# A searched start order, a shorter Newton step and casts on VectorE in a fused attention and MLP kernel

**Chip, cores, metric.** One core of one Trainium2 chip. The metric is the device time of one execution in microseconds (us), as the median of several executions. Lower is better. TensorE is called PE, its weight loads PEld, VectorE DVE, ScalarE ACT, GpSimd POOL, SyncE SP. An `ACTq`, `SPq` or `POOLq` line is an engine's queue of instructions, where it issues DMAs.

## The reference, cut to what matters

```python
q, k, v: (8 batches, 12 heads, 448 rows, 64)    g_q, g_k: (64,)
q_n = q / sqrt(mean(q*q) + 1e-6) * g_q          # the same for k with g_k
attn = softmax(q_n @ k_n.T / 8)                 # per head, 448 x 448
x = (attn @ v) in token order                   # 3584 x 768
h = x @ w_in                                    # w_in 768 x 2048
out = (h * sigmoid(1.702 * h)) @ w_out          # w_out 2048 x 768, out 3584 x 768, fp32
```

The input is random. A pair is two heads of one batch; a batch has six pairs, and the MLP of a batch can start only when all six are done.

## The kernel before

Every piece of work is a task with an engine, an estimated duration, what it depends on, and a key. While the program is built, a list scheduler walks through modelled time. On each engine it emits the ready task with the smallest key. On the chip only the order per engine and the semaphores remain: a modelled start time does not hold anything back there (c1_order below issued its first `w_in` chunk at 1.82 us, where its table of start times has 12.24).

The tasks of a pair `i` are named by letters: `L` loads, `S` square on ACT, `R` reduction on DVE, `Q0` and `Q` the reciprocal root by Newton's method, `N` norm, `T` turn (transpose) on PE, `KQ` and `K` copies of the turned rows out of PSUM (the memory in which PE leaves its results), `C` scores, `E` exponentials on ACT, `V` cast of the values, `P` their product, `O` division, `B` and `X` the turn back and its copy. `F` is a group of the first MLP product, `Y` of the second, `WI` and `WO` chunks of the weights.

```python
def rsqrt(grp):                        # DVE for pair 0, POOL for the others
    eng = nc.vector if grp[0] == 0 else nc.gpsimd
    eng.tensor_tensor(out=yf.bitcast(I32), in0=magic[:SS, :m], in1=t.bitcast(I32), op=ALU.subtract)
    for _ in range(2):                 # 1 + 2 x 4 operations
        eng.tensor_tensor(out=t, in0=yf, in1=yf, op=ALU.mult)
        eng.tensor_tensor(out=t, in0=t, in1=x, op=ALU.mult)
        eng.tensor_scalar(out=t, in0=t, scalar1=-0.5, scalar2=1.5, op0=ALU.mult, op1=ALU.add)
        eng.tensor_tensor(out=yf, in0=yf, in1=t, op=ALU.mult)

def norm(i, gi):                       # always POOL
    nc.gpsimd.tensor_tensor(out=row_ring[i % N_QKN]..., in0=raw[i]..., in1=y..., op=ALU.mult)

def vcast(i):                          # always POOL
    nc.gpsimd.tensor_tensor(out=vx[:, :, :D], in0=vr, in1=ones..., op=ALU.mult)

# ... the gains are loaded from SP's queue, keys such as i - 4.5 are set by hand,
# ... three PSUM banks rotate for turns and MLP groups, w_out comes in four chunks of 512 rows
od.add(("S", i, j), "ACT", 950 / len(parts) + 100, lambda ..., i - 4.5, deps=[("L", i, w) ...])
od.add(("F", b, m), "PE", KI * 189, lambda b=b, m=m: first(b, m), key,
       deps=[("X", b * NP + p) for p in range(NP)] + [("WI", m // 4), last], ...)
```

## Time and profile before

| | before |
|---|---|
| device time, median of 3 (lowest to highest) | 456.48 us (455.66 to 456.92) |
| span of the profiled run, granted clock | 455.0 us, 0.968 |
| first exponential | 14.36 us |
| first group of the first MLP product (called T below) | 59.72 us |
| end of PE's last matmul | 449.68 us |

T is the number to read. From T on PE has nearly no idle time (1.0 us in all), and from T to PE's end it takes 389.96 us. So the start is where this kernel can be shortened. A score group in PE's timeline (`sc`, 4 matmuls) is a handy thermometer: in before it takes 0.59 us at full clock (at 50.42) and 0.99 at half clock (at 44.34). I call PE warm at full clock and cold at half clock.

### The profile page before, as it was taken

To read this page: it belongs to the slowest core of one execution; us is meant where nothing else is said; L and a number is where in the kernel's file an instruction comes from. 1 tells how busy PE (TensorE), PEld (TensorE's weight loads), DVE (VectorE), ACT (ScalarE), POOL (GpSimd) and SP (SyncE) were. 2 spreads that over 40 slices of the span, in tenths; PEclk is the share of its full clock that TensorE was granted. 3 is DMA by queue.
4 is the path that set the end of the run, shared out by engine and by line. 5 is a ranking of instruction groups with operands and counts; after the bars stand their busy time and mean duration, and the time that the engine had idled before them with its cause. 6 is when DMAs were issued, how large, how long until landed. Compare 5 with 4: busy or idle time off the path is not lost.

```text
span 455.0 us, 9525 instructions
## 1 busy us (share of the span) xinstructions
PE 423.0 (93%) x3728; PEld 244.4 (54%) x3728; DVE 211.9 (47%) x453; ACT 319.2 (70%) x463; POOL 193.2 (42%) x309
## 2 busy tenths in 40 slices
PE   0676799999999999999999999999999999999995
PEld 0343555566555655556556655555556555565563
DVE  5664678864663347624564326632551135404400
ACT  4665798887887878877887878976786667514411
POOL 3997797565436364445445534535443000000000
PEclk9965789999999999999999999999999999999999
DMA  8999999787555875566738576454213431021022
GB/s 199 235 245 246 254 262 245 151 183 197 139 117 133 192 184 155 124 148 152 190 94 195 146 184 164 121 139 130 55 39 80 99 84 22 12 79 36 0 71 70
DMA packets 95341, 63.35 MB, mean 139 GB/s; under 512 B 54336, under 2 KB 91712, under 8 KB 95296
## 3 DMA queue, kind: packets, MB, share of 16 engines
q1 hardware_dynamic: 89808, 56.22, 51.0%
q0 software_dynamic: 5248, 6.29, 7.8%
q8 instruction: 29, 0.48, 0.4%
q10 hardware_dynamic: 240, 0.23, 0.2%
q14 instruction: 16, 0.13, 0.1%
HBM read 45.61 MB, written 11.01 MB: 124 GB/s over the span
## 4 chain that ended last, share of the span: by engine, by line
PE 86%; DMA 8%; DVE 2%; ACT 2%; SPq 1%; issue 0%; ACTq 0%; DVEq 0%
PE op L505 32%; PE gp L482 32%; PE o L345 12%; PE sc L334 10%; DMA raw<-in_k_dram 5%; DMA raw<-in_q_dram 2%; DMA gq<-in_g_q_dram 1%; ACT att L338 1%; DVE obs L356 1%; DVE ssq L252 0%; SPq L241 0%; PE ot_ps L368 0%; PE t_ps L305 0%; DVE g L497 0%; DVE rcp L355 0%
## 5 line engine op out<-in xcount | busy, mean ns | idle before, releaser
L338 ACT ACTIVATE att<-sc 112x896 bf16<-112x896 f32 x192 | 167.3, 914 | 22.3 <-PE sc L334 21.1
L505 PE MATMUL op<-w_out_s,g 128*128 128x384 bf16 x896 | 162.8, 326 | 0.0
L482 PE MATMUL gp<-xt,w_in_s 128*128 128x448 bf16 x768 | 160.5, 353 | 0.2
L289 POOL TENSOR_TENSOR row<-raw,rs 112x512 bf16<-112x512 f32 x96 | 98.0, 1043 | 40.9 <-DMA qk<-row 38.4
L345 PEld LDWEIGHTS <-att 112*128 112x128 bf16 x1536 | 79.2, 101 | 55.3 <-issue 23.3
L497 DVE SCALAR_TENSOR_TENSOR g<-th,gp 128x448 bf16<-128x448 f32 x128 | 78.5, 618 | 60.6 <-ACT th L491 60.4
L505 PEld LDWEIGHTS <-g 128*128 128x128 bf16 x896 | 79.7, 97 | 48.4 <-issue 4.4
L345 PE MATMUL o<-vx,att 112*128 112x65 bf16 x1536 | 95.2, 200 | 5.4 <-DVE obs L356 2.9
L482 PEld LDWEIGHTS <-w_in_s 128*128 128x128 bf16 x768 | 68.9, 98 | 57.9 <-issue 4.2
L491 ACT ACTIVATE th<-gp 128x448 f32<-128x448 f32 x128 | 69.8, 546 | 37.8 <-PE gp L482 37.4
L296 POOL TENSOR_TENSOR vx<-vraw,ones 112x512 bf16<-112x512 f32 x48 | 50.0, 1042 | 100.5 <-PE o L345 87.4
L252 DVE TENSOR_REDUCE ssq<-sq 112x16 f32<-112x1024 f32 (+1 forms) x50 | 58.6, 1174 | 38.9 <-ACT sq L246 36.7
L355 DVE RECIPROCAL rcp<-o 112x4 f32<-112x4 f32 x96 | 17.4, 181 | 105.9 <-PE o L345 105.5
L334 PE MATMUL sc<-qk 64*112 64x448 bf16 x384 | 61.3, 394 | 5.7 <-ACT att L338 4.3
L246 ACT ACTIVATE sq<-raw 112x1024 f32<-112x1024 f32 (+1 forms) x50 | 51.0, 1023 | 19.2 <-DMA raw<-in_k_dram 17.0
L515 ACT ACTIVATE osb<-op 128x384 f32<-128x384 f32 x56 | 27.4, 490 | 50.5 <-PE op L505 46.9
L356 DVE TENSOR_TENSOR obs<-o,rcp 112x256 bf16<-112x256 f32 x96 | 40.8, 425 | 3.3
L334 PEld LDWEIGHTS <-qk 64*112 64x112 bf16 x384 | 18.9, 131 | 22.8 <-issue 17.2
L324 ACT ACTIVATE qk<-qk,gG 128x448 bf16<-128x448 bf16 x36 | 24.1, 668 | 0.0
L305 PE MATMUL t_ps<-ident,row 112*128 112x112 bf16 x96 | 9.7, 262 | 12.9 <-POOL row L289 12.9
L305 PEld LDWEIGHTS <-row 112*128 112x128 bf16 x96 | 7.2, 123 | 15.9 <-POOL row L289 14.5
L276 POOL TENSOR_TENSOR rs<-magic,seed 112x48 int32<-112x48 int32 (+1 forms) x16 | 4.5, 280 | 23.3 <-DVE seed L267 20.9
(31 smaller groups left out, 78.8 us busy)
## 6 DMA issues: line engine op xcount, KB each, us to landing
raw<-in_q_dram SPq DMA_DIRECT2D x48, 224.0 KB, 3.8
vraw<-in_v_dram SPq DMA_DIRECT2D x48, 224.0 KB, 3.7
raw<-in_k_dram SPq DMA_DIRECT2D x47, 224.0 KB, 4.0
w_in_s<-in_moe_w_in_dram POOLq DMA_DIRECT2D x4, 768.0 KB, 13.5
w_out_s<-in_moe_w_out_dram POOLq DMA_DIRECT2D x4, 768.0 KB, 11.6
out_dram<-osb SPq DMA_DIRECT2D x8, 336.0 KB, 3.0
out_dram<-osb SPq DMA_DIRECT2D x8, 288.0 KB, 2.7
out_dram<-osb SPq DMA_DIRECT2D x8, 240.0 KB, 2.8
```

Source lines behind the costliest of these rows:

```text
L246: nc.scalar.activation(out=sq_of[i][:SS, part], in_=raw[i][:SS, part], func=ACT.Square)
L252: nc.vector.reduce_sum(out=ssq_of[g0][:SS, i - g0, part], in_=sq_of[i][:SS, part], axis=AX.X)
L289: nc.gpsimd.tensor_tensor(out=row_ring[i % N_QKN][:SS, gi].rearrange("p n (h d) -> p h n d", h=2), in0=raw[i][:SS, gi], in1=y[:SS, a, gi]. ...
L296: nc.gpsimd.tensor_tensor(out=vx[:, :, :D], in0=vr, in1=ones[:SS, :].to_broadcast([SS, 2 * NS, D]), op=ALU.mult)
L334: nc.tensor.matmul(sc[:SS, hp, :S], lhsT=qk_ring[i % N_KZ][r, 1, kc, :], rhs=qk_ring[i % N_KZ][r, 0], start=True, stop=True)
L338: nc.scalar.activation(out=att_ring[i % N_ATT][:SS, kc, :, :S], in_=scs.pop((i, kc))[:SS, :, :S], func=ACT.Exp)
L345: nc.tensor.matmul(os_[i, hp][:, qs, :], lhsT=att_ring[i % N_ATT][:SS, kc, hp, qs * SS:qs * SS + WIN], rhs=vx_ring[i % N_V][:SS, hp, kc, : ...
L356: nc.vector.tensor_tensor(out=obs[i][:SS, :, hp, :], in0=o[:SS, :, :D], in1=rcp[:SS, :].to_broadcast([SS, NS, D]), op=ALU.mult)
L482: nc.tensor.matmul(ps[:, :], lhsT=w_in_s[:, ki, m * 128:(m + 1) * 128], rhs=xT[b][:, ki, :], start=(ki == 0), stop=(ki == KI - 1))
L491: nc.scalar.activation(out=th[:, :], in_=gps[b, m][:, :], func=ACT.Tanh, scale=0.851)
L497: nc.vector.scalar_tensor_tensor(out=g_of[b // 2][:, m, lo:lo + S], in0=ths.pop((b, m))[:, :], scalar=1.0, in1=gps.pop((b, m))[:, :], op0= ...
L505: nc.tensor.matmul(ops[bp, tm, hf][:, :], lhsT=g_of[bp][:, ko, tm * 128:(tm + 1) * 128], rhs=w_out_s[:, ko, hf * HALF:(hf + 1) * HALF], st ...
```

## The change

The intent is to bring T forward. It has five parts, and two smaller edits that stand in the last line of the diff:

- The order of the first pairs was searched offline. The keys of some 300 tasks and the start times of the loads stand as tables in the kernel, and the scheduler's model of the DMA was refined for that search.
- Newton's step is shorter (six DVE operations instead of nine for pair 0), and pair 0 is normed on DVE.
- The values of pairs 0 to 5 are cast on DVE.
- `w_out` is loaded by column halves, and the gains from ACT's queue.
- A hook for filler matmuls is added with its factor at zero. So neither kernel runs any filler.

```diff
+    def fill(idle):                    # called ahead of each PE task until the first MLP group
+        for _ in range(int(idle * FILL / 110)):
+            nc.tensor.matmul(banks[2][:, :256], lhsT=ident[:, :], rhs=zeros[:, :], start=True, stop=True)
+    FILL = 0.0
+        t.key = KEYS.get(name, key)    # KEYS and AT: two tables, about 80 lines, cut here
+        t.after, t.at, t.takes = tuple(deps), AT.get(name, at), takes
 ... seed: the halving and the sign are folded into two tensor_scalar, rsqrt:
         for _ in range(2):
-            eng.tensor_tensor(out=t, in0=yf, in1=yf, op=ALU.mult)
+            eng.tensor_tensor(out=t, in0=yg, in1=yg, op=ALU.mult)
             eng.tensor_tensor(out=t, in0=t, in1=x, op=ALU.mult)
-            eng.tensor_scalar(out=t, in0=t, scalar1=-0.5, scalar2=1.5, ...)
-            eng.tensor_tensor(out=yf, in0=yf, in1=t, op=ALU.mult)
+            if eng is nc.vector:
+                eng.scalar_tensor_tensor(out=yg, in0=t, scalar=1.5, in1=yg, op0=ALU.add, op1=ALU.mult)
+                continue
 ... norm
-        nc.gpsimd.tensor_tensor(
+        eng = nc.vector if i == 0 else nc.gpsimd
+        eng.tensor_tensor(
 ... vcast
+        if i < NP:
+            nc.vector.tensor_copy(out=vx[:, :, :D], in_=vr)
+            return
 ... load_g
-                nc.sync.dma_start(out=t[lo:lo + 64, :], ...)
+                nc.scalar.dma_start(out=t[lo:lo + 64, :], ...)
 ... load_out: hf, r = c // 2, c % 2
-            out=w_out_s[:, 4 * c:4 * c + 4, :],
+            out=w_out_s[:, 8 * r:8 * r + 8, hf * HALF:(hf + 1) * HALF],
 ... the turn is split into its two halves; two PSUM banks rotate before the first MLP group, three after
```

## The prediction

> **What bounds the kernel now.** I read the page's shares first, then its slices, then a table of stretches, then the timelines of the stretch that stood out.
>
> ```profile
> PE 423.0 (93%) x3728; PEld 244.4 (54%) x3728; DVE 211.9 (47%) x453; ACT 319.2 (70%) x463; POOL 193.2 (42%) x309
> ...
> PE   0676799999999999999999999999999999999995
> ...
> PEclk9965789999999999999999999999999999999999
> DMA  8999999787555875566738576454213431021022
> ```
>
> PE is full from the seventh slice on. The loss is in the first six slices (to 68 us) and in the last. The stretches, whose columns after the window are length, then PE, weight loads, DVE, ACT and POOL busy, granted clock, DMA share and GB/s:
>
> ```profile
> 30.00:40.00 10.00, 6.97 (x80) 5.49 (x78) 5.37 (x16) 2.04 (x3) 7.37 (x9) 0.50 1.18 245
> 40.00:50.00 10.00, 6.99 (x59) 4.05 (x58) 3.61 (x10) 7.34 (x10) 9.24 (x17) 0.50 1.16 256
> ...
> 100.00:150.00 50.00, 49.88 (x457) 28.50 (x456) 25.30 (x54) 40.61 (x61) 23.84 (x37) 1.00 0.61 146
> ```
>
> From 100 us PE is the bound and nothing else matters. From 30 to 50 us PE has few instructions, at half clock, and ACT is nearly idle. PE's timeline shows when the MLP starts:
>
> ```profile
> 59.37 0.56 PE L368 MATMUL ot_ps<-ident,obs 112*128 112x112 bf16 x4
> 59.72 1.73 PE L482 MATMUL gp<-xt,w_in_s 128*128 128x448 bf16 x6
> ```
>
> The first gp group needs the transposed outputs of all six pairs of batch 0; the sixth arrives at 59.4. From there MLP work fills every gap, and PE has under 2 us of idle time until it ends at 449.7. So the end is the start of the MLP plus fixed PE work plus a fixed 5.3 us tail. ACT's timeline says why the start is so late:
>
> ```profile
> 27.24 3.35 ACT L338 ACTIVATE att<-sc 112x896 bf16<-112x896 f32 x4
> 35.83 1.06 ACT L246 ACTIVATE sq<-raw 112x1024 f32<-112x1024 f32 x1 [5.24 <-DMA raw<-in_k_dram]
> 39.60 1.06 ACT L246 ACTIVATE sq<-raw 112x1024 f32<-112x1024 f32 x1 [2.71 <-DMA raw<-in_k_dram]
> 40.56 1.70 ACT L338 ACTIVATE att<-sc 112x896 bf16<-112x896 f32 x2
> ```
>
> These are the exponentials of pair 2, then two squares, then the exponentials of pair 3. The scores of pair 3 were ready at about 36.3 us, but ACT takes its work in order and stood at squares of later pairs, whose keys had not landed. The static order was made with wrong landing times. Before that, pair 3 itself was late: its norm on POOL starts at 28.3, after a Newton step shared with pairs 4 and 5, while the first w_in chunks (issued at 15.8 and 21.9) shared a saturated DMA with the loads. Two smaller losses:
>
> ```profile
> 7.73 0.17 DVE L283 TENSOR_TENSOR rs<-rs,seed 112x16 f32<-112x16 f32 x1
> 7.93 1.01 DVE L279 TENSOR_TENSOR seed<-rs 112x16 f32<-112x16 f32 x1
> ...
> 2.68 1.22 SPq L387 DMA_DIRECT2D gq<-in_g_q_dram  x2
> 3.94 1.36 SPq L387 DMA_DIRECT2D gk<-in_g_k_dram  x2
> ```
>
> A 0.17 us DVE operation takes 1.01 while POOL's first cast of values runs (7.88 to 8.92), and issuing the gains keeps SP from the loads of pair 2 for 2.6 us.
>
> [...] two score groups take 0.99 us at 13.7 and at 44.3, against 0.59 at 50.4. [...] POOL's norm is 1042 ns here[...]. [...] about 245 GB/s whichever queues are active up to 80 us.
>
> **The change part by part.** PE's work is not changed: no matmul goes, and the filler's factor is zero (before has none either). What can move is the MLP's start, T, now 59.7 us.
>
> 1. First pair. Its queries and keys are squared and reduced by 6.47. Now seed (0.4), Newton (8 operations, 2.6 us[...]), then two norms on POOL, 9.66 to 11.75. Then: seed 0.4, Newton in six DVE operations of about 0.2 (1.25), two norms on DVE (1.2): done at about 9.4, and the first half is transposed while the second is normed. First exponential at about 11.2 instead of 14.36: 3 us. The gains go to ACT's queue, so pair 2 is issued 2.6 us earlier.
>
> 2. The order. I count ACT, which has most to do before T. A pair needs four exponentials (3.33 us) and a square (0.95). From 11.2: 24 exponentials, 20.0; squares of pairs 3 to 5, 2.9 (0 to 2 fit in the gap before 11.2); some three squares of batch 1 in between, 2.9. The last exponential of pair 5 then ends at 37.0 against 55.1 now. The order of before has done squares up to pair 11 by that time; three of these, 2.9 us, now come later. From the last exponential to the first gp group 4.6 us pass now, partly at half clock with pair 6 interleaved; halves of values 0.9, divide 0.6, transpose and copy 0.65 and semaphores make 3. T is 40, and I add 1 for leftover gaps: T = 41.
>
> 3. Values cast on DVE for six pairs: six POOL operations of 1.04, 6.2 us off POOL[...]. POOL then needs for batch 0: ten norms 10.4, two Newton groups 4.5, four w_in issues 3.7. It isn't the bound. The Newton step on POOL has eight operations instead of nine, some 0.3 us per group, hidden.
>
> 4. Feed. A pair's load of 229 KB takes 0.94 us at 245 GB/s. The software queue had 7.8% of 455 us for eight weight chunks, 4.4 us each. Batch 0 and w_in are 18 x 0.94 + 4 x 4.4 = 34.5, from about 2.5: 37 us. That fits T = 41, as the last w_in chunk isn't needed until some 14 us later. The second product starts 29.5 us after T now (89.2), so at about 70; adding half of w_out (8.8) and batch 1 (16.9) to 37 gives 63. This is where the column halves count: by rows the first output tile needs all four chunks (71.5, too late); by halves three tiles of 2.6 us come before the other two chunks.
>
> Sum: 59.7 - 41 = 18.7. I give back 1 because fewer scores and turns of batch 1 are done at T (before had nine turns and seven pairs' scores), and 0.7 for short stalls after T. Net 17: 456.5 - 17 = 439.5.
>
> **The rivals.** (a) PE at half clock becomes the bound in place of ACT. A pair at half clock is turns 0.8, scores 1.9, values 2.0, back-turn 0.4: 5.1 us, above ACT's 4.3. Six from 9.3 end at 40, plus 3 is 43, more with stalls. [...] Result: about 442. (b) The order was searched with modelled times; where DMA lands later, ACT again stands in front of a square. Half of the gain goes: 447. For it: that is what happened to before. Against it: the new model shares the DMA between two queues and holds loads back to set times, aimed at just this. (c) After T the feed is short: w_out or pairs 9 to 11 late, PE idles for some us between 55 and 85, and part of the 18.7 comes back as waits of gp or op: 443 to 446. My sums leave only some 7 us of room at 70. (d) Everything fits and the search packs better than my count: T near 36, 434. (e) PE was the bound in the first 60 us anyway, or two PSUM buffers instead of three before T hold it up: no gain. PE's few instructions from 30 to 50 speak against it.
>
> **Range and chances.** 439.5 us; (d) sets the low end and (b) or (c) the high end: 433 to 447.5. The 2% line lies at 447.4, a gain of 9.1, half of what I count; I hold faster at 0.90, within 2% at 0.08, slower at 0.02.
>
> **What would show it.** First exponential at 11 to 12 us. ACT with no wait over 2 us in front of a square between 15 and 37. First gp at about 41; PE busy at least 9.5 of 10 from 50 on, and after the first gp the same PE time to the end (some 390 us) within 3. First op at about 70 with no DMA in front. The tail after PE's end 5.3. The step on T is wrong if gp starts outside 36 to 45; that on the feed if PE has more than 3 us idle after T. If T moves by the full 18 and the end doesn't, my reading that PE alone sets the rest is wrong.

## The result, and the profile after

Ratios here are the mean time of one kernel's fast runs over the mean of the other's fast runs of the same rounds, so not quite the ratio of the medians quoted beside them. Intervals are 95%.

| | before | after |
|---|---|---|
| median of 4 (lowest to highest) | 456.18 (455.66 to 456.92) | 454.13 (453.49 to 454.62) |
| ratio | 1 | 0.9953 [0.9933, 0.9973] |
| first exponential | 14.36 | 15.87 |
| T | 59.72 | 56.27 |
| PE's end | 449.68 | 446.41 |
| T to PE's end | 389.96 | 390.14 |

The change gains 2 us, not 17. It is within 2%, and 454.13 is outside the predicted range. From T on everything went as predicted: 390.14 us of PE work, then the 5.3 us tail. But T came 15.3 us later than predicted. (The profiled execution of after is the fastest of its four, 453.49, and that of before took 456.74, so T differs by 3.5 us here where the medians differ by 2.)

These are parts 1 and 2 of the page of after, to be held against the first fence of the prediction:

```profile
PE 424.7 (94%) x3728; PEld 246.3 (55%) x3728; DVE 215.8 (48%) x458; ACT 319.5 (71%) x463; POOL 185.2 (41%) x285
...
PE   0599699999999999999999999999999999999995
...
PEclk9999799999999999999999999999999999999999
```

PE's row now has 9s from the third slice (22.6 us) with a dip in the fifth, and the clock row shows 9s nearly throughout. Read alone, both rows say that the start has become dense and warm. The stretches of after say the same (columns as in the prediction's table):

```profile
20.00:30.00 10.00, 9.01 (x82) 5.50 (x83) 7.80 (x19) 8.04 (x10) 8.63 (x15) 1.00 1.17 245
30.00:40.00 10.00, 9.29 (x101) 6.47 (x100) 6.48 (x14) 5.87 (x7) 5.42 (x6) 1.00 1.18 243
40.00:50.00 10.00, 8.24 (x92) 5.38 (x89) 7.87 (x19) 9.87 (x12) 4.41 (x11) 1.00 1.17 259
50.00:60.00 10.00, 7.69 (x61) 4.62 (x62) 5.59 (x14) 3.17 (x6) 9.26 (x13) 0.66 1.16 257
```

PE is busy 9.01 and 9.29 of 10, where before had 7.92 and 6.97. But ACT is busy only 5.87 in the second of these. PE's own timeline shows why a busy PE delivers little:

```profile
15.21 0.99 PE L487 MATMUL sc<-qk 64*112 64x448 bf16 x4 [0.54 <-DVE qk L466]
...
38.83 0.99 PE L487 MATMUL sc<-qk 64*112 64x448 bf16 x4
...
51.94 0.56 PE L459 MATMUL w<-ident,row 112*128 112x112 bf16 x4 [2.03 <-POOL row L439]
...
55.35 0.99 PE L487 MATMUL sc<-qk 64*112 64x448 bf16 x4
56.27 3.00 PE L645 MATMUL w<-xt,w_in_s 128*128 128x448 bf16 x12
```

Every whole score group (x4) from 15.21 to 43.11 takes 0.99 us or more, and every half group (x2) 0.62. That is half clock, although the clock column says 1.00. The first clock event that the kept trace holds starts at 47.2 us, and the column counts time without an event as 1.00, so durations must decide. For the same reason the mean clocks of two kernels can't be compared. PE becomes warm at 47.2, waits 2.03 us for a POOL norm, and is cold from 50.6 to 57.4, so again at T. In front of T also stand turns and scores of batch 1, which T doesn't need. (In after, `w<-xt,w_in_s` is the group that before called `gp`.) ACT's timeline, after the first exponential:

```profile
27.39 3.59 ACT L491 ACTIVATE att<-sc 112x896 bf16<-112x896 f32 x4 [0.98 <-PE sc L487]
...
39.55 3.65 ACT L491 ACTIVATE att<-sc 112x896 bf16<-112x896 f32 x4 [1.63 <-PE sc L487]
...
56.01 1.73 ACT L491 ACTIVATE att<-sc 112x896 bf16<-112x896 f32 x2 [5.80 <-PE sc L487]
```

The waits in front of squares are gone (5.1 us for keys in the whole run against 17.0). In their place ACT waits for PE's scores. The last wait starts after the last exponential of batch 0 and costs T nothing; the earlier ones sum to 5.9 us. DVE's timeline shows the first pair:

```profile
7.35 0.16 DVE L533 TENSOR_TENSOR gG<-gq,gk 128x1 f32<-128x1 f32 x1 [0.73 <-DMA gk<-in_g_k_dram]
...
7.62 0.68 DVE L401 TENSOR_REDUCE ssq<-sq 112x8 f32<-112x512 f32 x1
...
9.88 2.40 DVE L401 TENSOR_REDUCE ssq<-sq 112x16 f32<-112x1024 f32 x3
12.20 0.68 DVE L439 TENSOR_TENSOR row<-raw,rs 112x512 bf16<-112x512 f32 x1
...
16.59 1.10 DVE L447 CAST vx<-vraw 112x512 bf16<-112x512 f32 x1
```

The gains' product stands ahead of pair 0's second reduction and waits for its DMA. Three reductions of pairs 1 and 2 (2.40 us) stand between Newton's last operation and pair 0's first norm.

### The profile page after: what moved, and what is told of

It reads as the page before. It is cut to its first block, busy times and chain, and to the rows that moved or that the text cites. A ratio compares the mean times of both kernels' runs of the same rounds, so it can differ in the third digit from the quotient of the medians.

```text
span 451.7 us, 9527 instructions
## 1 busy us (share of the span) xinstructions
PE 424.7 (94%) x3728; PEld 246.3 (55%) x3728; DVE 215.8 (48%) x458; ACT 319.5 (71%) x463; POOL 185.2 (41%) x285
## 4 chain that ended last, share of the span: by engine, by line
PE 91%; DMA 2%; DVE 2%; ACT 1%; POOL 1%; issue 0%; SPq 0%; ACTq 0%; POOLq 0%
PE w L668 33%; PE w L645 32%; PE o L498 13%; PE sc L487 11%; DMA raw<-in_k_dram 1%; PE w L459 1%; DMA gq<-in_g_q_dram 1%; PE w L521 1%; ACT att L491 1%; DVE obs L509 1%; ACT sq L395 0%; POOL row L439 0%; DVE vx L447 0%; DVE ssq L401 0%; DVE rcp L508 0%
## 5 line engine op out<-in xcount | busy, mean ns | idle before, releaser
L668 PE MATMUL w<-w_out_s,g 128*128 128x384 bf16 x896 | 161.6, 326 | 0.0
L645 PE MATMUL w<-xt,w_in_s 128*128 128x448 bf16 x768 | 159.0, 353 | 0.1
L660 DVE SCALAR_TENSOR_TENSOR g<-th,w 128x448 bf16<-128x448 f32 x128 | 78.9, 618 | 64.5 <-ACT th L654 64.1
L498 PEld LDWEIGHTS <-att 112*128 112x128 bf16 x1536 | 77.5, 102 | 48.4 <-issue 21.8
L654 ACT ACTIVATE th<-w 128x448 f32<-128x448 f32 x128 | 69.9, 546 | 37.1 <-PE w L645 35.3
L449 POOL TENSOR_TENSOR vx<-vraw,ones 112x512 bf16<-112x512 f32 x42 | 43.8, 1044 | 119.2 <-PE o L498 107.6
L498 PE MATMUL o<-vx,att 112*128 112x65 bf16 x1536 | 91.9, 200 | 0.7 <-DVE obs L509 0.4
L401 DVE TENSOR_REDUCE ssq<-sq 112x16 f32<-112x1024 f32 (+1 forms) x50 | 58.5, 1174 | 27.8 <-ACT sq L395 26.5
L678 ACT ACTIVATE osb<-w 128x384 f32<-128x384 f32 x56 | 27.5, 491 | 50.8 <-PE w L668 49.1
L459 PE MATMUL w<-ident,row 112*128 112x112 bf16 x96 | 11.0, 268 | 15.6 <-DVE row L439 12.9
L425 POOL TENSOR_TENSOR t<-rs 112x48 f32<-112x48 f32 (+1 forms) x32 | 8.8, 277 | 32.5 <-DVE rs L414 30.0
```

Source lines behind the costliest of these rows:

```text
L401: nc.vector.reduce_sum(out=ssq_of[g0][:SS, i - g0, part], in_=sq_of[i][:SS, part], axis=AX.X)
L449: nc.gpsimd.tensor_tensor(out=vx[:, :, :D], in0=vr, in1=ones[:SS, :].to_broadcast([SS, 2 * NS, D]), op=ALU.mult)
L498: nc.tensor.matmul(os_[i, hp][:, qs, :], lhsT=att_ring[i % N_ATT][:SS, kc, hp, qs * SS:qs * SS + WIN], rhs=vx_ring[i % N_V][:SS, hp, kc, : ...
L645: nc.tensor.matmul(ps, lhsT=w_in_s[:, ki, m * 128:(m + 1) * 128], rhs=xT[b][:, ki, :], start=(ki == 0), stop=(ki == KI - 1))
L654: nc.scalar.activation(out=th[:, :], in_=gps[b, m], func=ACT.Tanh, scale=0.851)
L660: nc.vector.scalar_tensor_tensor(out=g_of[b // 2][:, m, lo:lo + S], in0=ths.pop((b, m))[:, :], scalar=1.0, in1=gps.pop((b, m)), op0=ALU.ad ...
```

## The experiments

Two theories stood at the start. The first, H, says that PE's half clock holds T back: warm the PE, and T moves far forward. Its rival says that the order itself (or the first pair, the gains' issue, or the casts on DVE) sets T whatever the clock. Where an expectation speaks of a plan or a model, it means the start times that the kernel's own list scheduler assigns while it builds the program. They are no measurements, and the argument doesn't rest on them. All fourteen runs gave correct results (a1_again is a1_fill's file once more). Each has 4 runs; the kernel before has 7.

The table collects the positions from the timeline of each profiled run:

| run | median (lowest to highest) | ratio to before [95%] | first exp. | T | T to PE's end |
|---|---|---|---|---|---|
| a1_fill | 447.34 (447.10 to 448.56) | 0.9819 [0.9777, 0.9860] | 15.71 | 51.90 | 389.6 |
| a1_again | 446.93 (446.85 to 447.09) | 0.9788 [0.9758, 0.9818] | 15.53 | 49.58 | 390.4 |
| a2_nosearch | 456.60 (455.30 to 458.46) | 1.0027 [0.9981, 1.0072] | 17.84 | 55.64 | 394.6 |
| a3_gains | 454.47 (451.28 to 456.59) | 0.9971 [0.9907, 1.0035] | 19.48 | 59.44 | 390.3 |
| a4_casts | 454.88 (453.87 to 455.20) | 0.9982 [0.9945, 1.0019] | 15.72 | 57.40 | 390.6 |
| b1_nosearch_fill | 454.06 (453.32 to 455.52) | 0.9933 [0.9889, 0.9976] | 18.66 | 53.02 | 394.0 |
| b2_fill_start | 451.65 (450.28 to 453.46) | 0.9870 [0.9812, 0.9929] | 15.29 | 55.09 | 390.7 |
| b3_rows | 448.01 (447.14 to 448.85) | 0.9818 [0.9780, 0.9856] | 15.32 | 49.46 | 390.6 |
| c1_order | 459.01 (454.69 to 459.58) | 1.0017 [0.9956, 1.0077] | 23.87 | 58.83 | 393.7 |
| c2_order_nofill | 455.94 (454.06 to 458.03) | 0.9971 [0.9913, 1.0029] | 23.20 | 56.83 | 394.5 |
| d1_tail | 450.26 (449.63 to 451.84) | 0.9866 [0.9830, 0.9902] | 15.49 | 46.40 | 396.0 |
| d3_first | 447.31 (447.05 to 447.42) | 0.9796 [0.9765, 0.9826] | 15.98 | 50.26 | 390.1 |
| e2_keys_only | 448.58 (448.09 to 449.06) | 0.9832 [0.9792, 0.9873] | 15.19 | 51.89 | 389.2 |
| e3_squares | 449.20 (448.87 to 452.68) | 0.9860 [0.9810, 0.9909] | 15.15 | 46.48 | 395.2 |

### Fillers on: a1_fill, and the same file again

```diff
-    FILL = 0.0
+    FILL = 0.8
```

The hook then puts matmuls of zeros (256 columns each, into an unused PSUM bank) wherever the model sees PE idle before the first MLP group: 83 ahead of the first turn, and about 110 in later gaps. Nothing else changes.

> The changed kernel with the filler factor at 0.8 in place of 0: dummy matmuls of 256 columns of zeros in the idle time that the order's own model sees on PE (some 83 before the first turn, some 110 in the gaps up to the first gp group); order of real work unchanged. Theory H (half clock): in the changed kernel PE is nearly solid from 20 to 48 us, with score groups of 0.99 us as in a cold array, so it sets the pace there; kept warm, score groups take 0.59, and the first gp group comes at 47 to 51 us instead of 56.3; time some 5 to 8 us lower, 446 to 449. Rival R (order and waits): PE's solid row is only stretched to fill the waits for ACT and DVE; with a warm array the same waits appear as gaps, the first gp group stays at 54 to 57, time within 2 us of 454.1, or longer if the fillers get in the way.

> The kernel with the filler at 0.8 once more, so that the next three have it on their own chip: 446 to 449 us, first gp group at 51 to 53.

The two runs gave 447.34 and 446.93. Relative to the change's own ratio the first is 0.9819/0.9953 = 0.9866 and the second 0.9788/0.9953 = 0.9834, that is 6.1 and 7.5 us of 454.1. These are stretches and PE's timeline of a1_again:

```profile
20.00:30.00 10.00, 9.79 (x130) 6.28 (x131) 8.75 (x21) 8.71 (x11) 8.96 (x16) 1.00 1.17 242
30.00:40.00 10.00, 9.85 (x147) 6.85 (x146) 7.68 (x18) 9.41 (x12) 6.92 (x7) 1.00 1.18 245
```

```profile
15.09 0.58 PE L487 MATMUL sc<-qk 64*112 64x448 bf16 x4
...
49.06 0.59 PE L487 MATMUL sc<-qk 64*112 64x448 bf16 x4
49.58 2.44 PE L645 MATMUL w<-xt,w_in_s 128*128 128x448 bf16 x12
```

Score groups take 0.58 and 0.59 all along, ACT is busy 9.41 of 10 between 30 and 40 instead of 5.87, and T is at 49.58. PE does more work (the fillers) and is done sooner. So H holds for 6.7 us of T (56.27 - 49.58; 4.4 in the profile of a1_fill), and the end follows it. H does not hold for the rest: with a clock of 1.00 throughout, T is still 8.6 later than the predicted 41. In a1_fill one filled gap came out too short: PE waited 1.98 us at 46.46, the clock of that stretch fell to 0.85, and T was 51.90. So T differs by 2.3 us between two profiles of one file. The profiled execution of a1_fill was the slowest of its four (448.56); the medians are 0.4 apart.

### The order without its search: a2_nosearch, and with fillers b1_nosearch_fill

```diff
-        t.after, t.at, t.takes = tuple(deps), AT.get(name, at), takes
+        t.after, t.at, t.takes = tuple(deps), at, takes
-        t.key = KEYS.get(name, key)
+        t.key = key
```

b1 has `FILL = 0.8` besides.

> The changed kernel without the table of searched keys and start times (the rule's own keys and times instead); all other parts stay. If the search is what the gain of 2 us comes from, this is at 456 or above and its first gp group at 58 to 62 us. If the other parts bring the gain, it stays near 454 and 56 us. The order's own model puts the first gp group at 49.6 us here against 49.2 with the search, and the second product at 84 against 75.7.

> The changed kernel without the searched keys and times, but with the filler at 0.8 as in the run before that gained. Theory: with a warm array the first gp group comes when the order allows it. If the searched order is worth something once the array is warm, this is slower than the searched order with the filler (447.3 us, first gp group at 51.9): 449 to 452. If the filler alone is what counts and the order is nothing, 447 to 448.

Without the search T is at 55.64, no later than with it, though the first exponential is 2 us later. The loss lies after T. From T to PE's end it takes 394.6 us instead of 390.1, for instance PE is busy 18.65 of 20 between 80 and 100, where after has 19.78. Up to 0.9 us of the 4.4 is half clock, which lasts 3.0 us beyond T here (to 58.6) and 1.2 in after. So while PE is cold, the search gains nothing at T and 4.4 us after it. In time that is about 3 us here: 1.0027/0.9953 = 1.0074 of 454.1.

With fillers on both, the searched order is worth 5.2 to 6.6 us: 454.06 against 447, that is 0.9933/0.9819 to 0.9933/0.9788. The search was made with durations nearer to a warm PE (its model counts 320 ns for a score pair; a1_again shows 0.40 us warm, after 0.62 cold). That it is worth more on a warm PE is therefore plausible but not shown: 3 and 5 to 7 us are not told apart by these intervals.

### Where the gains are issued: a3_gains

```diff
-                nc.scalar.dma_start(out=t[lo:lo + 64, :], ...)
+                nc.gpsimd.dma_start(out=t[lo:lo + 64, :], ...)
```

In after, ACT issues the gains for 2.45 us (1.20 to 3.65), and its table load moves from 1.19 to 3.69. I wanted that back.

> The changed kernel with the gains loaded from POOL's queue, idle then, in place of ACT's; all orders unchanged. In the changed kernel ACT's table load starts at 3.69 us, behind 2.5 us of issuing the gains, and the first square at 5.28. Theory F (the start of the first pair carries through): the table load starts at about 1.2, the first square at about 4.5, the first exponential 0.7 us or more earlier than 15.87, and the first gp group and the time fall by as much. Rival: the first pair waits for its norm on DVE behind three reductions (to 12.2 us), so that nothing moves by more than 0.3 us.

The table load did go back to 1.20. But the first square then waited for its data, and the gains landed late by this queue, as ACT's and DVE's timelines of a3_gains show:

```profile
5.07 0.63 ACT L395 ACTIVATE sq<-raw 112x512 f32<-112x512 f32 x1 [2.60 <-DMA raw<-in_k_dram]
...
10.95 0.16 DVE L533 TENSOR_TENSOR gG<-gq,gk 128x1 f32<-128x1 f32 x1 [4.53 <-DMA gk<-in_g_k_dram]
...
11.22 0.68 DVE L401 TENSOR_REDUCE ssq<-sq 112x8 f32<-112x512 f32 x1
```

The first square starts at 5.07 instead of 5.28, so the late table load costs 0.2 us at most. Pair 0's second reduction stands behind the gains' product and starts at 11.22 instead of 7.62. The first exponential came 3.6 us later, T 3.2 later, and the profiled span 2.8 longer (454.5 against 451.7). The expected gain did not come. In this one execution, with the opposite sign, a shift of the first pair reaches the end nearly undiminished when the rest of the order stays. That is not shown for the kernel: two of its runs took about 456.4, the profiled one among them, and two 451.28 and 452.66, less than after's median.

### Casts back on POOL: a4_casts

```diff
-        if i < NP:
-            nc.vector.tensor_copy(out=vx[:, :, :D], in_=vr)
-            return
```

> The changed kernel with the values of the first six pairs cast on POOL as before, at the same places in the order; all else unchanged. If the casts on DVE are a gain: POOL's norms come later, first gp group 1 to 3 us later than 56.3. If they cost (the DVE casts took 1.10, 1.25 and 1.68 us beside POOL's norms, against 0.42 alone, and one of them stands ahead of the copy of a pair's keys): the first gp group comes 0.5 to 2 us earlier and the time falls by as much.

T was 57.40, 1.1 later. The time, 0.9982 [0.9945, 1.0019] against 0.9953, is not told apart. So the casts on DVE are a small help at most, and they are not where the gain was lost. On DVE they took 0.42 us where no POOL norm ran and 1.10 to 1.68 beside one, such as at 16.59 in the fence above.

### Fillers only before the first turn: b2_fill_start

```diff
-        for _ in range(int(idle * FILL / 110)):
+        for _ in range(int(idle * FILL / 110) if idle > 5000 else 0):
```

(With `FILL = 0.8`.) If the solid real work keeps a warmed PE warm, the fillers in the gaps are superfluous.

> The changed kernel with the filler only ahead of the first turn (83 dummy matmuls), none in the gaps. Theory H with a clock that falls back: score groups start at 0.59 us at 15 us and go back to 0.99 before 30, as the work by itself has gaps; first gp group at 53 to 56, time 450 to 453. If a warm array stays warm on the real work alone, this equals the run with all fillers: 447 to 448 and 52 us.

It gave 451.65, between the two. The stretches, and three groups of PE's timeline:

```profile
20.00:30.00 10.00, 9.55 (x91) 6.04 (x92) 7.77 (x17) 7.97 (x10) 8.99 (x15) 0.50 1.18 239
30.00:40.00 10.00, 9.50 (x95) 6.31 (x92) 5.75 (x16) 6.33 (x8) 5.17 (x6) 0.50 1.18 245
```

```profile
14.86 0.59 PE L487 MATMUL sc<-qk 64*112 64x448 bf16 x4 [0.54 <-DVE qk L466]
...
22.49 0.99 PE L487 MATMUL sc<-qk 64*112 64x448 bf16 x4
```

Here the record itself says 0.50, with PE busy 9.55 and 9.50 of 10. The recorded clock of the warmed PE falls at 16.5 us, after some gaps of 0.5 to 0.8 us. None of them is long, but together they left PE busy for only 1.25 of the 3.41 us before the fall. Then it stayed at half clock until 43.8, though it was hardly ever idle. Two things follow. The half clock of after is real, not a misreading of durations. And the early warm-up alone did not keep the clock: with the fillers in the gaps as well, in a1_again, score groups stayed at 0.58 and 0.59 us. (Gap fillers without the early ones were not run.)

### An order searched anew: c1_order and c2_order_nofill

I searched new keys and start times with the scheduler's own model, and ran the result with fillers (c1) and without (c2). The tables are most of the edit (over 200 lines). The model's durations are changed too, and ACT's table load, the issue of the gains and the issue of pair 0's keys are now tasks of ACT that take its time. c2 is c1 with `FILL = 0.0`.

> Another searched order, with the filler at 0.8: the order's model now counts the ACT table load and the issue of the gains as ACT's time, 0.86 us for an exponential, 0.96 us for a load and 4.7 for a weight chunk; it puts no square ahead of the last exponentials of pair 5 and no turns of batch 1 ahead of the first gp group. Its plan has the first gp group at 45.4 us; the plan of the changed kernel had 49.2 and the run with the filler showed 51.9. If what is left of the shortfall is order, the first gp group comes at 46 to 49 and the time is 441 to 445; if DMA lands later than the model has it and ACT stands again, 50 to 52 and 446 to 448.

> The same other order without any filler. Theory H: the array runs at half clock, PE is solid again from about 20 us and the first gp group comes at 51 to 55 us whatever the order plans; time 6 to 9 us above the same order with the filler, so 449 to 453. Rival R: the order is what counts, and it comes within 2 us of the run with the filler.

Both failed. The first exponential came at 23.87 and 23.20. ACT's timeline of c1:

```profile
5.50 0.37 ACTq L398 DMA_DIRECT2D raw<-in_k_dram  x1
13.20 1.15 ACT L403 ACTIVATE sq<-raw 112x512 f32<-112x512 f32 x2 [8.02 <-DMA raw<-in_k_dram]
```

In this order ACT issues pair 0's keys only at 5.50, behind its first square. POOL issues the first chunk of `w_in` at 1.82, since nothing on the chip holds it to the later start time of the model, 12.24 us, and its 768 KB are loaded beside what pair 0 needs (169 GB/s in all from 0 to 10 us). The second square waits 8.02 us. H's expectation of a gain from fillers missed here too: c1 is not faster than c2 (459.01 and 455.94, both spread by about 4 us). With a late first pair the fillers, placed by modelled gaps, stood in PE's way: one block of 22 ran from 18.91 for 4.58 us, ahead of the first scores at 23.43, whose rows were ready at 21.3. So fillers placed by a wrong model held these scores back by some 2 us; in time the two kernels are not told apart.

### Only what T needs before T: d1_tail, and its parts e2_keys_only and e3_squares

On top of `FILL = 0.8`, d1 makes squares and reductions of pairs 9 to 11 wait for the last exponential and the last copy of batch 0, and the turns of pairs 6 to 8 for the second MLP group. With the searched keys of pairs 6 to 9 the scheduler then finds no task that can start, and the build stops, so d1 has the hand-set keys for these.

```diff
+KEYS = {n: v for n, v in KEYS.items() if n == "gG" or n[0] in ("L", "WI", "WO") or n[1] < 6}
-                   + [("R", i - N_SQ, 0), ("R", i - N_SQ, 1)])
+                   + [("R", i - N_SQ, 0), ("R", i - N_SQ, 1)]
+                   + ([("E", 5, 3)] if i in (9, 10, 11) else []))
-                   lambda i=i, p=part: reduce(i, p), i - 4.3, deps=[("S", i, j)])
+                   deps=[("S", i, j)] + ([("X", 5)] if i in (9, 10, 11) else []))
 ... turns
+                       + ([("F", 0, 1)] if i in (6, 7, 8) else [])
```

> The filler at 0.8, and what stands ahead of the first gp group without being needed for it moved behind: squares and reductions of pairs 9 to 11 behind the last exponentials and copies of batch 0, turns of pairs 6 to 8 behind the second gp group, pairs from 6 on in their natural order. Rule of the prediction (only the start of the MLP counts, PE is full after it): first gp group at 47.5 to 49.5 instead of 51.9, and the time falls by the same 2.5 to 4 us, to 443.5 to 445. Rival (the feed): batch 1 comes late, PE idles before the second batch's gp groups at 80 to 110 us, and the time is 446 to 452 in spite of the earlier start. The order's own model says the rival: second product at 83.6 instead of 75.7, its end 4 us later.

T moved forward by 3.2 us, to 46.40, and the time got 3.3 us longer (450.26 against 446.93). PE's timeline behind T:

```profile
46.40 2.44 PE L652 MATMUL w<-xt,w_in_s 128*128 128x448 bf16 x12
...
51.83 0.59 PE L491 MATMUL sc<-qk 64*112 64x448 bf16 x4 [2.60 <-DVE qk L470]
```

After two MLP groups PE turns pair 6 and waits 2.60 us for the copies of its rows. From T to PE's end it takes 396.0 us instead of 390.4. PE also becomes cold: the fillers end at T, and the recorded clock is 0.50 from 53.0 to 56.4 us, which costs up to 1.7 us, estimated as half of these 3.4. But d1 changed the keys besides postponing work, and the runs without any search also need 394 us behind T. So two more runs took it apart, each on top of `FILL = 0.8`: e2 has only the filter on the keys, and e3 has all searched keys and only the two changes to squares and reductions.

> Filler factor 0.8 and the searched keys kept only for pairs 0 to 5, with nothing postponed: the part of the run d1 that I had not looked at by itself. If d1 gave its start back because batch 1 was fed late, this run keeps about 390 us from the first MLP group to PE's end, with that group at about 49.6, and a time of about 447 like the filled kernel. If the loss behind the first MLP group is that of the hand-set keys of pairs 6 to 9, as in the two runs without any search (394 us), this run takes 394 to 396 us from that group to PE's end and about 451.

> Filler factor 0.8, all searched keys kept, only the squares and reductions of pairs 9 to 11 held back behind the last exponential and the last copy of batch 0; the turns of pairs 6 to 8 stay where they are. If work ahead of the first MLP group that this group does not need costs its full time there, the group comes 1 to 2 us earlier than 49.6 and, with 390 us behind it, the time is about 445.5. If that work only fills waits of ACT, the group stays within 0.5 us of 49.6 and the time at 447 or, where pairs 9 to 11 are then missed, 448 to 450 with more than 391 us behind the group.

The keys alone (e2) cost no time behind T: 389.2 us. T itself is 2.3 later, at 51.89, and the time is 448.58. The postponed squares alone (e3) bring T to 46.48 and take 395.2 us behind it. So postponing these squares is enough for the loss behind T (e3's clock stays at 1.00 there). PE's waits of e3 from 46 to 150 us, after the name of the waiter: total, times, longest:

```profile
PE sc L487 <- ACT att L491: 1.0, 2, 0.6
PE w L521 <- DVE obs L509: 1.0, 2, 0.7
PE w L647 <- DVE qk L466: 0.6, 1, 0.6
PE o L498 <- DVE obs L509: 0.6, 1, 0.6
...
```

With the two cut lines they sum to 4.0 us, where a1_again has 0.8 in the same stretch. The remaining 1.6 of the 4.8 is mostly work that only changed sides: between 46.57 and T, a1_again does turns and a score group of batch 1 (0.37 + 0.37 + 0.57 + 0.59 us), of which e3 has only one turn of 0.37 ahead of its T. So a gain at T is no gain at the end by itself. In these four filled kernels T varies from 46.4 to 51.9, and PE's end only from 439.9 to 442.4. The prediction's rule, end is T plus a constant, holds only for kernels whose order is the same around T.

### Pair 0's norms ahead of the reductions: d3_first

On top of `FILL = 0.8`, the three reductions and the seed of pairs 1 and 2 are emitted right after pair 0's second norm:

```diff
+        late = [self.named[n] for n in (("R", 2, 0), ("R", 1, 0), ("R", 1, 1), ("Q0", 2))]
+        at = log.index(self.named[("N", 0, 1)]) + 1
+        log[at:at] = late              # log: the tasks in emission order, emitted at the end
```

> The filler at 0.8, and on DVE only the reductions of pairs 1 and 2 (and the seed of their group) moved behind the two norms of pair 0; nothing else in any order. In the run with the filler the norms waited 2.4 us behind three reductions (9.84 to 12.15). If the first pair's chain carries through: first exponential at 13.3 to 13.8 instead of 15.7, first gp group 1 to 2 us earlier, time 445.5 to 446.5. Rival: pair 1 then comes later by the same amount (its Newton step waits for these reductions), the gap only moves behind pair 0's exponentials, and the first gp group stays within 0.5 us of 51.9.

DVE's timeline:

```profile
10.25 1.29 DVE L450 TENSOR_TENSOR row<-raw,rs 112x512 bf16<-112x512 f32 x2
11.46 2.40 DVE L412 TENSOR_REDUCE ssq<-sq 112x16 f32<-112x1024 f32 x3
...
14.20 0.38 DVE L474 COPY qk<-w 128x448 bf16<-128x448 bf16 x1
```

Both norms are done at 11.5 instead of 13.8, but the same 2.40 us now stand in front of the copy of the turned rows. The first exponential came at 15.98, no earlier, and the time is that of a1_again within 0.4 us. The gap only moved. I have not run an order with the reductions behind the copies as well; then pairs 1 and 2 would come later. It would also need other fillers: here those ahead of the first turn hold it until 12.57, though its norm is done at about 10.9.

### w_out by rows again: b3_rows

On top of `FILL = 0.8`, `load_out` loads 512 rows per chunk, as before did.

```diff
-            out=w_out_s[:, 8 * r:8 * r + 8, hf * HALF:(hf + 1) * HALF],
+            out=w_out_s[:, 4 * c:4 * c + 4, :],
```

> The filler at 0.8, and w_out loaded by rows as before instead of by column halves; issue times and all orders unchanged. If the halves are needed once the MLP starts early: the second product, at 77.9 us, waits for the last chunk (issued at 64.6, some 14 us to land) and the time rises by 1 to 3 us. If the feed has room: within 0.5 us of the kernel with the filler.

448.01 against 446.93, T at 49.46, the first group of the second product at 76.45 against 76.30 and without a wait for a DMA. The halves are worth about 1 us at most, which is within the noise (a1_fill, with halves, has the same ratio as b3_rows).

## Why the prediction was wrong, step by step

**Right for this change: what bounds the kernel.** In after, T plus the fixed time gives the end: 390.14 us after T (389.96 before), tail 5.3. The miss is in T alone, 56.27 instead of 41, which is 15.3 us. As a rule it is too strong: e2 and e3 differ by 5.4 us in T and by 0.6 in PE's end. The 0.7 and 1 us that I gave back for short stalls and for less of batch 1 done were the right terms. How large they are depends on what is moved: a1_again gives back 0.2 for an advance of 6.7, and e3, which postpones squares, 4.8 for a further 3.1.

**Wrong: step 1, the first pair.** First exponential 15.87 instead of 11.2, so 4.7 late. Newton itself is as counted (8.32 to 9.96, 1.64 us for 0.4 + 1.25; before's step has nine operations, not eight), and the norms are near it (0.68 each against 0.6, which was my estimate; on POOL a norm took 1.04 in before). What I mis-sized is what stands around them. Pair 0's sums were ready at 8.30 instead of 6.47, 1.8 late. One half of that is its data: its second square ends at 6.66, where before had 5.64. The other half is the gains' product, which waits for its DMA ahead of the second reduction (7.62). Three reductions of the next pairs then take 2.3 us between Newton and the first norm. I had counted DVE's work for pair 0 as if DVE had none for pairs 1 and 2. d3_first shows that moving them behind the norms does not help.

The step also said that pair 2 would be issued 2.6 us earlier. It was issued still earlier, but for another reason: in the searched order its queries are SP's first load (0.74, before 5.34), ahead of those of pair 0 (1.19), and its keys the third (1.68, before 5.97). SP is not freed by moving the gains: it then waits 3.1 us for pair 0's keys to land, and its fourth load is at 5.27. That the loads of pair 2 are what delays pair 0's data was not tested by itself.

**Wrong: step 2, ACT as the bound, and the dismissal of rival (a).** From the first exponential to T I counted 29.8 us, and it took 40.4. Rival (a) had PE at half clock as the bound, and I set it aside, because I expected a busy PE to come to full clock as it had in before at 50 us (0.99 us for a score group at 47.62, 0.59 at 50.42). That was my assumption. In after PE did not, for some 26 us (20.6 to 47.2) at about 90% busy. a1_again shows what that costs: with a warm PE the same stretch takes 34.05 us, so 6.35 of the 10.6 are half clock. The other 4.25 were in the count: between the first and the last exponential ACT does seven squares instead of the six that I counted, 1.0 us. Its waits take 3.0 us, and the way from the last exponential to T takes 4.3 us even when warm, against 4 with the leftover.

So the 15.3 are 4.7 for the first pair, 6.4 for half clock and 4.2 for an order that is not as tight as ACT's work alone. Rival (a)'s own number, 442, was too low too, since it started from my first exponential, let the half-clock work run without gaps, and left out the turns and scores of batch 1 that stand ahead of T.

**Rival (b) fell.** ACT does not stand in front of squares any more; the search did what it was made for. It exchanged that wait for the wait for scores. **Rivals (c) and (d)** did not show: PE waits for no DMA after T, and T is late. **Rival (e)** said that PE was the bound before T anyway, or that two PSUM buffers hold it up. Its result, no gain, came close; the two buffers were not tested, since every run but before has them.

**Right: step 3, but small.** A DVE cast took longer beside a POOL norm (1.10 to 1.68 us against 0.42), and a4_casts puts the whole at 1.1 us of T, within noise in time.

**Right: step 4, the feed.** The second product starts at 82.80, 26.5 us behind T, with no DMA in front, and b3_rows shows that the halves were hardly needed. But the count was for a second product at 70, and so early it never came: the earliest in a run is 76.30, in a1_again. So the room that the step counted was not put to the test.

**Open.** The runs do not settle why PE's real work from 20 to 46 us does not release the clock. In before it was released at 23.0 and at 50.3, with less solid work (PE busy 4.92 of 10 us from 10 to 20 and 6.99 from 40 to 50, though for 100% and 99% of the last 3.41 us), and in a1_again, with matmuls of zeros in the gaps, score groups stayed at 0.58 and 0.59 us. The kept traces of before and after show more about the fall than about the release. Up to 75 us the recorded changes of the clock come at 23.03, 26.45, 50.34, 57.17 and 60.58 in before and at 47.20, 50.62 and 57.44 in after, each 3.41 us or a multiple of it behind the one before. In the 3.41 us ahead of the three falls PE was busy for 47% and 61% (before, to 26.45 and to 57.17) and 39% (after, to 50.62), and in b2_fill_start for 1.25 of the 3.41 us. In before the clock held after 77% (50.3 to 53.8) and 78% (67.4 to 70.8). For the release the same figures do not agree: after 3.41 us at 98% it did not come (after, 26.7 to 30.1), after as long at 92% it did (before, 57.2 to 60.6). What releases the clock is not shown by busy time, and what share of it makes the clock fall is not shown beyond these cases. Nor is it settled how much earlier the end could come with an order that advances T and still feeds batch 1: d1_tail and e3_squares show only that postponing its squares gives more back than it gains. The split turn and the two PSUM buffers of the change were in every run but before, so their share is not known.

The best version that I ran is the change with `FILL = 0.8`, at 446.93 and 447.34. It beats both kernels, by 2% of before at the point estimate (the intervals reach from 0.9758 to 0.9860, so across the 2% line).

## What to carry to other kernels

When PE's share rises and its output doesn't, read the durations of one repeated matmul group before trusting a clock column or a busy row: here a nearly full PE at half clock looked like a gain. The searched order was worth about 3 us here with a cold PE and 5 to 7 with a warm one, and dummy matmuls in its gaps were worth three times what the change gained by itself (6 to 7.5 us against 2). Before taking work out from in front of a milestone, ask who needs it just behind the milestone: what you gain there can come back as a wait.
